# RetNet attention and squared-ReLU FFN on one core: the two row halves of a chunk ordered by TensorE's wait on itself, and three steps of an ending block left between the two parts of x

## The chip, the cores and the metric

The kernel runs on one core of a Trainium2 chip, in one launch. The metric is the device time in microseconds; the median of the runs shown counts. The profile is one profiled execution: its span, from the first to the last instruction, was 984.6 us, and that run's time was 986.41 us.

The engines are called by their names or as the profile has them: TensorE (PE for the matmuls, PEld for the loads of the stationary operand), VectorE (DVE), ScalarE (ACT), GpSimd (POOL) and SyncE (SP, whose queue issues nearly all DMAs).

## The reference

Batch 8, 8 heads, 576 positions, head size 64; then an FFN over 4608 tokens, 512 to 2048 to 512. q, k and v are float32, the weights float64 (the kernel rounds them itself), and the result is float32.

```python
scores = scale * np.matmul(q, k.transpose(0, 1, 3, 2))
Dmat = np.where(rel >= 0, gamma[:, None, None] ** rel[None, :, :], 0.0)
ret = scores * Dmat[None, :, :, :]
attn = np.matmul(ret, v)                 # (B, H, S, D)
x = attn.transpose(0, 2, 1, 3).reshape(B * S, H * D)
h = np.maximum(x @ w_in, 0.0)
out = h * h @ w_out
```

## The kernel before

**Two phases.** In the first phase the attention is computed chunk by chunk, and between the chunks the first product of the FFN, for blocks of 512 tokens, is worked off in small steps. In the second phase, from about 580 us on, only the second product of the FFN remains (`inner`, L1033). The change touches the first phase alone.

**Chunks.** A sequence of 576 positions is cut into four chunks of 128 and one of 64; there are 40 chunks, numbered i. A chunk of 128 has two halves h of 64 positions. The decay allows a recurrent form: within a half the masked scores are multiplied with v ("own", `own_of`, L566), what all earlier halves leave is kept as a 64x64 state u for each head ("grow", `grow_of`, L556, which accumulates in PSUM and is copied out to `u_sb` by `grown`, L491 on ScalarE), and q times that state is added (L609). The results of own and of L609 accumulate in the same PSUM tile, `x_ps`, which holds all heads of a chunk and has one buffer.

**Row halves.** All these matmuls are 64x64 and use TensorE as four tiles of 64x64. Which rows of the array a matmul uses is set by the partitions of its operands: for own it is half h of the positions (`rows(h)`), for L609 it is one of the two heads of a pair (`rows(e)`). [...] In `whole` (L587), which does one chunk from the eleventh on, the order is: own and grow of half 0 in two parts (`beside_each` with `(0, 2)` and then `(4, 6)`), half of the next chunk's scores (L451), the matmuls of L609, own and grow of half 1 `(0, 2)`, the other half of the next scores, own and grow `(4, 6)`. Two waits stand in it: the first matmul of L609 must come after the end of the first part of own, and the last part of own after the last matmul of L609. The wait is made by `seen` (L576) and `after` (L572): ScalarE copies one column of a small tile `mark` (L577) once the awaited matmul is done, and the later matmul waits for that copy.

**x and the blocks.** `x_out` (L532) copies a chunk's `x_ps` into `xT` (L544 on ScalarE). `xT` holds x transposed, for two blocks of 512 tokens at a time. A chunk can lie across a block's boundary: the boundaries at tokens 2048, 3072 and 4096 fall into the middle of a chunk, those at 2560 and 3584 between two chunks. Where a chunk lies across, there are two copies: the first completes block n and puts the steps of block n on the list, the second begins block n + 1. Block n + 1 lies where block n - 1 was, so before that copy the loop at L541 works off all steps that block n - 1 still has.

**Steps.** A block has 28 steps (`ffn_in`, L703): for each of four groups of weights the seven products of a Strassen-like scheme, j = 0 to 6, into the PSUM tiles h_a, h_b, h_c (L718). Each product is evacuated by ScalarE (L728, L734) or VectorE (L730, L732, L737, L741, L744, with the squaring L725), on GpSimd A11 is squared (L735), and the sums L658 and L659 and the write of g to DRAM (L660, on SP's queue) are put on a list and done one by one in later steps. The first step (j = 0) needs x as it is; the second needs T2, the second of four sums over x that VectorE makes in `sum_x` (L637): L644, L645, L646, L647. If block n + 1 has its x by then, one of the four is made in each of the steps j = 3, 4, 5 of block n's last group (L748); the rest, or all of them, at step 0 of block n + 1. VectorE further does a piece of the conversion of w_out (L201 to L248, loaded at L196, written at L281) in most steps.

**Pace.** `ffn` (L802) is called for each chunk and decides how many steps come before the next chunk: it interpolates between points of `PACE` (L796), pairs of tokens gone and steps done. In the steps it also issues the transposes of q and k for a chunk two further (`flips`, L398 on VectorE, which waits for the load of k, L148 and L150) and the copies of these into place (`move`, L410, with L413 on ScalarE). Before each chunk `move(C, i)` issues what that chunk still lacks.

**Order.** The program is scheduled by hand (`manual_schedule`): each engine does its instructions in the order of the Python code. A wait of one instruction holds all later ones on the same engine.

Of the kernel before, what the change touches and what calls it, by code (L numbers as in the profile page):

```python
# [9 lines left out]
F32 = mybir.dt.float32  # L10
# [5 lines left out]
C = 128  # L16
CH = C // 2
TOK = 512
# [22 lines left out]
def kernel(  # L41
# [33 lines left out]
    nc = tc.nc  # L75
# [10 lines left out]
    N_MP = N_M // 2  # L86
    N_MQ = N_M // 2
    N_BLK = n_tok // TOK
    NP = len(PRODUCTS)
# [4 lines left out]
    const = ctx.enter_context(tc.tile_pool(name="const", bufs=1))  # L94
# [226 lines left out]
            f and f()  # L321

    dv = only.tile([128, H, 2 * NCH], F32, name="dv")
    mark = const.tile([128, 2], F32, name="mark")
    nc.vector.memset(mark, 0.0)
    exp_bias = const.tile([128, 1], F32, name="exp_bias")
    nc.gpsimd.memset(exp_bias, -896.0 * 2.0 ** 23)
    idle, ident = (W[6][:, at:at + 128] for at in (2688, 2816))
# [30 lines left out]
    def rows(half, n=64):  # L359
        return slice(64 * half, 64 * half + n)  # L360
# [7 lines left out]
    def clears(half, bank):  # L368

        new = (half, bank) not in clean  # L370
        clean.add((half, bank))
        return new
# [10 lines left out]
    N_ONE = N_TURN - 1  # L383
# [26 lines left out]
    def move(count, i=N_CH):  # L410

        while moves and count and moves[0][0] <= i and (moves[0][1] <= done[0] or count == C):
            nc.scalar.copy(*moves.pop(0)[2:])  # L413
            count -= 1
# [15 lines left out]
    def scores(i, part=False):  # L430

        b_, ci, c0, cs = chunks[i]
        if i < N_EARLY:

            sc = [ps_f.tile([128, 512], F32, tag="f", name="sc_ps")[:, 0:256].rearrange("p (h t) -> p h t", h=HP) for e in range(2)]
        else:
            both = ps_t.tile([128, 2, 512], F32, tag="t", name="sc_ps")[:, :, 0:256].rearrange("p e (h t) -> p e h t", h=HP)
            sc = [both[:, e, :, :] for e in range(2)]
        st[i]["sc"] = sc
        st[i]["both"] = None if i < N_EARLY else both  # L440
        if part:
            return
        for hp in range(HP):
            score(i, hp)
        masked(i)

    def score(i, hp):
        for h in range(chunks[i][3] // CH):
            for e in range(2):
                t = slice(CH * h, CH * h + CH)  # L450
                nc.tensor.matmul(st[i]["sc"][e][rows(h), hp, :], lhsT=st[i]["kT"][rows(e), hp, t], rhs=st[i]["qT"][rows(e), hp, t],  # L451
                                 start=True, stop=True, skip_group_check=True)

    def masked(i):

        b_, ci, c0, cs = chunks[i]
        sc, both = st[i]["sc"], st[i]["both"]
        r = st[i]["ret"] = st[i]["kT"].rearrange("p (e a) (b t) -> p e (a b) t", e=2, b=2)
        if i < N_EARLY:
            for e in range(2):  # L460
                nc.vector.tensor_tensor(r[:cs, e, :, :], sc[e][:cs], msk[:cs, 0, :, :].to_broadcast([cs, HP, CH]), op=ALU.mult)
        else:
            nc.vector.tensor_tensor(r[:cs], both[:cs], msk[:cs].to_broadcast([cs, 2, HP, CH]), op=ALU.mult)
        if i < N_ONE:
            scale_v(i)
# [7 lines left out]
    def x_at(hp, b, h):  # L473
        return xp[0][rows(b), hp // 2, 0:256].rearrange("p (g t) -> p g t", g=2)[:, hp % 2, CH * h:CH * h + CH]
# [15 lines left out]
    def grown(i, h):  # L490
        nc.scalar.copy(u_sb[(2 * chunks[i][1] + h + 1) % 3], u_ps[0])  # L491
# [40 lines left out]
    def x_out(i, after):  # L532

        b_, ci, c0, cs = chunks[i]
        tok = b_ * S + c0
        at = tok
        p = xp[0][:, :, 0:256].rearrange("p a (g t) -> p a g t", g=2)
        while at < tok + cs:
            n = at // TOK

            while steps and steps[0][0] <= n - 2:  # L541
                step()
            end = min(tok + cs, (n + 1) * TOK)
            nc.scalar.copy(xT[n][:, :, at - n * TOK:end - n * TOK].rearrange("p (a g) t -> p a g t", a=2),  # L544
                           p[:, :, :, at - tok:end - tok])
            if at == tok:
                after()
            at = end
            if n_next[0] < N_BLK and (n_next[0] + 1) * TOK <= at:
                steps.extend(block_steps(n_next[0]))  # L550
                n_next[0] += 1
        st[i] = loaded[i] = None
# [3 lines left out]
    def grow_of(i, h):  # L556

        ci = chunks[i][1]
        if ci == 0 and h == 0:
            u_ps[0] = ps_u.tile([128, HP, D], F32, tag="u", name="u_ps")  # L560
        u = u_ps[0]
        return [lambda hp=hp, e=e, b=b: nc.tensor.matmul(
            u[rows(e), hp, :], lhsT=loaded[i][1][rows(h), 2 * hp + e, :], rhs=st[i]["vs"][rows(h), 2 * hp + b, :],
            start=(ci == 0 and h == 0 and hp == 0), stop=(hp == HP - 1), skip_group_check=True) for hp, e, b in HEADS]

    def own_of(i, h):  # L566
        s = st[i]
        return [lambda hp=hp, e=e, b=b: nc.tensor.matmul(
            x_at(hp, b, h), lhsT=s["vs"][rows(h), 2 * hp + b, :], rhs=s["ret"][rows(h), e, hp, :],
            start=clears(b, hp // 2), stop=False, skip_group_check=True) for hp, e, b in HEADS_1]  # L570

    def after(later, earlier):  # L572
        tc.add_manual_dep(later.ins, earlier.ins.name,
                          mybir.DependencyInfo(mybir.DependencyClass.Sync, mybir.DependencyReason.DATA), reason="row halves")

    def seen(done_):  # L576
        a = nc.scalar.copy(mark[:, 1:2], mark[:, 0:1])  # L577
        after(a, done_)
        return a

    def beside_each(own, grow, js):
        made = []
        for j in js:
            made.extend(f() for f in own[j:j + 2] + grow[j:j + 2])
        return made

    def whole(i):  # L587

        b_, ci, c0, cs = chunks[i]
        s = st[i]  # L590
        xp[0] = ps_x.tile([128, 2, 256], F32, tag="x", name="x_ps", padded_shape=[128, 2, 512])
        clean.clear()
        more = ci + 1 < NCH
        out_of, into = own_of(i, 0), grow_of(i, 1) if more else []
        f1 = seen(beside_each(out_of, into, (0, 2))[-1])
        beside_each(out_of, into, (4, 6))
        if more:
            grown(i, 1)
        if i + 1 < N_CH:
            scores(i + 1, True)  # L600
            score(i + 1, 0)
            score(i + 1, 1)
        f2 = None
        for h in range(cs // CH):
            if 2 * ci + h == 0:
                continue
            u = u_sb[(2 * ci + h) % 3]
            for hp, e, b in HEADS[0:2] + HEADS[4:6] + HEADS[2:4] + HEADS[6:8]:
                m = nc.tensor.matmul(x_at(hp, b, h), lhsT=u[rows(e), hp, :], rhs=s["qT"][rows(e), hp, CH * h:CH * h + CH],  # L609
                                     start=clears(b, hp // 2), stop=False, skip_group_check=True)  # L610
                if f1:
                    after(m, f1)
                    f1 = None
        if cs == C:
            f2 = seen(m)
        grows = i + 1 < N_CH and chunks[i + 1][3] == C
        out_of, into = own_of(i, 1) if cs == C else [], grow_of(i + 1, 0) if grows else []
        beside_each(out_of, into, (0, 2))
        if i + 1 < N_CH:
            score(i + 1, 2)  # L620
            score(i + 1, 3)
            masked(i + 1)
        last = beside_each(out_of, into, (4, 6))
        if f2:
            after(last[0], f2)
        x_out(i, lambda: grown(i + 1, 0) if grows else None)


# [149 lines left out]
    def block_steps(n):  # L778
        if n == 0:
            seconds = [(0, first_in, j, (1,)) for j in range(N_HALF)]  # L780
            return seconds + [(0, first_in, j) for j in range(N_HALF, N_W1)]
        return [(n, ffn_in, n, mp, j) for mp in range(N_MP) for j in range(NP)]

    def step():
        n, f, *args = steps.pop(0)
        done[0] += 1
        f(*args)
# [5 lines left out]

    HALF = C // 2
    N_0 = N_W1
    PACE = ((4 * TOK, N_0 + 2 * N_MP * NP), (5 * TOK - HALF, N_0 + 3 * N_MP * NP - 2),  # L796
            (6 * TOK, N_0 + 4 * N_MP * NP), (8 * TOK, N_0 + 6 * N_MP * NP), (9 * TOK, N_0 + 7 * N_MP * NP - 2))
    done = [0]
    gone = [0]
    behind = []  # L800
# [1 line left out]
    def ffn(i, half):  # L802
# [13 lines left out]
        if not behind:  # L816
            behind.append((gone[0] - HALF, done[0]))
        points = behind + [p for p in PACE if p[0] > behind[0][0]]
        want = points[-1][1]
# [378 lines left out]
```

## Time and profile before

| | us |
|---|---|
| median of 3 runs | 986.56 |
| lowest and highest | 984.46, 989.82 |
| span of the profiled execution | 984.6 |
| TensorE matmuls busy | 956.0 |
| weight loads busy | 858.1 |
| VectorE busy | 783.9 |
| ScalarE busy | 346.5 |
| GpSimd busy | 127.9 |

The profile's page has the busy time of each engine, the span in 40 slices, the DMA queues, the chain that ended last, the costliest groups of instructions and the DMA issues. Of a group it gives line, engine, operation, the tiles written and read with their shapes, the count, then the busy time and the mean of one, and the idle time just before with what ended it. Beside the page there are views on the trace: busy times by stretches, who waited for whom, and the instructions in order of time (start, length, engine, line, operation, tiles, count; in brackets the idle time before and what ended it). Rows of the timeline are merged: "x16" is sixteen instructions in a row, from the first's start to the last's end.

Two things to keep in mind. Matmuls are pipelined and their ends are modelled, so a matmul row can cover a short hole; the rows of weight loads show such a hole better. And the time of the whole is an average over stages: the first 127 us (weights converted, chunks one by one), the stage from 127 to 532 us in which `whole` runs, the rest of the first phase, and the second phase.

### The profile page before, as it was taken

Reading aid. Unit: us, or ns where it says so; the run is one execution under the profiler, and the core shown is the slowest. Engines: PE = TensorE matmul, PEld = TensorE weight load, DVE = VectorE, ACT = ScalarE, POOL = GpSimd, SP = SyncE. Lnnn points to the kernel's source line nnn. Section 1 sums busy time; section 2 is a strip of 40 time slices with the busy share of each in tenths; the row PEclk is TensorE's granted clock in tenths of the full one; section 3 lists DMA queues with packets and bytes.
Section 4 is the critical chain, followed back from the end, with each engine's and each line's share of the span. In section 5 each row is a group of like instructions: output and inputs, shape, how many; then the busy total and the mean of one; then the engine's idle time right before and its main releaser. Section 6 shows DMA issues by size and latency. Waiting matters only on the chain. (4 is left out here: it accounts for less than half of the span.)

```text
span 984.6 us, 24068 instructions
## 1 busy us (share of the span) xinstructions
PE 956.0 (97%) x10108; PEld 858.1 (87%) x10108; DVE 783.9 (80%) x1448; ACT 346.5 (35%) x872; POOL 127.9 (13%) x121
## 2 busy tenths in 40 slices
PE   7799989999999999999999999999999999999998
PEld 7645778888878878888788889999999999999998
DVE  4789779887897778878786577878878787787876
ACT  3454366665774856665651000000000000000000
POOL 3211223122122221321200000000000000000000
PEclk9999999999999999999999999999999999999999
DMA  8875537575746764596229976645352544534241
GB/s 203 235 216 156 160 99 208 155 246 187 219 141 214 214 192 146 153 290 190 84 104 377 345 257 240 232 152 200 109 204 108 183 178 170 202 126 171 87 172 44
DMA packets 172012, 181.43 MB, mean 184 GB/s; under 512 B 118144, under 2 KB 132480, under 8 KB 165248
## 3 DMA queue, kind: packets, MB, share of 16 engines
q1 hardware_dynamic: 169792, 179.38, 56.5%
q8 instruction: 79, 1.29, 0.5%
q10 hardware_dynamic: 2112, 0.52, 0.2%
q14 instruction: 29, 0.24, 0.1%
HBM read 109.36 MB, written 70.52 MB: 183 GB/s over the span
## 5 line engine op out<-in xcount | busy, mean ns | idle before, releaser
L718 PE MATMUL h_b<-room,w 128*128 128x256 f32 x768 | 185.7, 385 | 11.3 <-DVE room L645 7.9
L718 PEld LDWEIGHTS h_b<-room,w 128*128 128x128 f32 x768 | 146.1, 192 | 34.3 <-issue 9.8
L413 ACT COPY qk<-flip 32x256 f32<-32x256 f32 x416 | 167.3, 402 | 6.0
L1047 PE MATMUL o_b<-w,room 128*128 128x128 f32 x1168 | 144.4, 275 | 0.2 <-DVE room L999 0.2
L1047 PEld LDWEIGHTS o_b<-w,room 128*128 128x128 f32 x1168 | 137.2, 192 | 0.4 <-DVE room L999 0.4
L1047 PE MATMUL o_c<-w,room 128*128 128x128 f32 x1008 | 123.0, 275 | 0.0
L718 PE MATMUL h_a<-room,w 128*128 128x256 f32 x512 | 122.9, 383 | 0.0
L718 PE MATMUL h_c<-room,w 128*128 128x256 f32 x512 | 122.3, 382 | 0.0
L1047 PEld LDWEIGHTS o_c<-w,room 128*128 128x128 f32 x1008 | 117.7, 192 | 0.0
L1061 ACT COPY r<-o_a 128x128 f32<-128x128 f32 x53 | 14.1, 266 | 271.9 <-PE o_a L1047 236.2
L718 PEld LDWEIGHTS h_c<-room,w 128*128 128x128 f32 x512 | 97.6, 192 | 13.9 <-DVE room L744 0.2
L718 PEld LDWEIGHTS h_a<-room,w 128*128 128x128 f32 x512 | 95.7, 190 | 14.0 <-issue 0.5
L1047 PE MATMUL o_a<-w,a 128*128 128x128 f32 x688 | 85.6, 275 | 0.0
L1047 PEld LDWEIGHTS o_a<-w,a 128*128 128x128 f32 x688 | 81.2, 192 | 0.1
L725 DVE SCALAR_TENSOR_TENSOR room<-room 128x512 f32<-128x512 f32 x96 | 74.0, 770 | 3.3
L735 POOL TENSOR_TENSOR room<-room 128x512 f32<-128x512 f32 x32 | 34.4, 1076 | 319.6 <-ACT room L734 282.2
L682 PE MATMUL h_ps<-room,w 128*128 128x512 f32 (+1 forms) x152 | 58.9, 535 | 3.4 <-DVE w L228 2.5
L377 POOL TENSOR_TENSOR q_ld<-q_ld,dv 128x512 f32<-128x512 f32 (+1 forms) x39 | 43.3, 1109 | 112.4 <-DMA q_ld<-in_q_dram 87.4
L737 DVE TENSOR_TENSOR room<-h_b,room 128x512 f32<-128x512 f32 x32 | 22.0, 688 | 44.9 <-PE h_b L718 44.9
L470 POOL TENSOR_TENSOR v_ld<-v_ld,dv 128x512 f32<-128x512 f32 (+1 forms) x40 | 50.7, 1268 | 22.8 <-DMA v_ld<-in_v_dram 16.4
L682 PEld LDWEIGHTS h_ps<-room,w 128*128 128x128 f32 x152 | 27.6, 190 | 26.1 <-issue 23.3
L1047 PE MATMUL o_b<-w,a 128*128 128x128 f32 x344 | 45.6, 275 | 0.0
(112 smaller groups left out, 1389.0 us busy)
## 6 DMA issues: line engine op xcount, KB each, us to landing
g_dram<-room SPq DMA_DIRECT2D x32, 1280.0 KB, 5.5
a<-g_dram SPq DMA_DIRECT2D x30, 1024.0 KB, 6.0
room<-g_dram SPq DMA_DIRECT2D x15, 1024.0 KB, 6.0
w<-w_dram SPq DMA_DIRECT2D x7, 1792.0 KB, 10.5
out_dram<-room SPq DMA_DIRECT2D x17, 512.0 KB, 3.3
w<-in_moe_w_in_dram SPq DMA_DIRECT2D x16, 512.0 KB, 5.6
w<-in_moe_w_out_dram SPq DMA_DIRECT2D x16, 512.0 KB, 4.0
v_ld<-in_v_dram SPq DMA_DIRECT2D x31, 256.0 KB, 3.4
```

What stands on the lines that cost most here:

```text
L377: engine.tensor_tensor(t, t, dv[:cs, :, NCH + ci:NCH + ci + 1].to_broadcast([cs, H, D]), op=ALU.mult)
L413: nc.scalar.copy(*moves.pop(0)[2:])
L470: nc.gpsimd.tensor_tensor(vs[:cs], vs[:cs], dv[:cs, :, ci:ci + 1].to_broadcast([cs, H, D]), op=ALU.mult)
L682: nc.tensor.matmul(p.rearrange("p h t -> p (h t)"), lhsT=w[:, c, :], rhs=xT[0][:, c, lo * HT:hi * HT], start=(c == 0), stop=(c == N_DM - 1))
L718: nc.tensor.matmul(p[:, mm, :], lhsT=w[:, c, :], rhs=xs[n][right][:, c, :], start=(j in OPENS and mm == 0 and c == 0), stop=(j in CLOSES a ...
L725: nc.vector.scalar_tensor_tensor(t, t, 0.0, t, op0=ALU.max, op1=ALU.mult)
L735: nc.gpsimd.tensor_tensor(g["A11"], g["A11"], g["A11"], op=ALU.mult)
L737: nc.vector.tensor_tensor(g["A22"], p, p15, op=ALU.add)
L1047: nc.tensor.matmul(p, lhsT=s["lefts"][left][:, m, :], rhs=w_out[j][:, m, WO_SLOT[right], :], start=(i in OPENS and m == 0), stop=(i in CLO ...
L1061: nc.scalar.copy(r[:, 0, 0:128], p)
```

## The change

Three parts:

1. `seen`, `after` and the tile `mark` go. In their place `wait_for` (a `nop` on TensorE that depends on the awaited matmul) stands ahead of L609 and ahead of the last part of own. The awaited matmuls are the same as before.
2. The loop in `x_out` that works off an ending block now issues two copies (`move(2)`) before each step, for chunks from the eleventh on.
3. Three points of `PACE` change: at tokens 2048, 3072 and 4096 the steps wanted were all those of the ending block; now they are two fewer, and the point lies 16 tokens later. In the order of the built kernel this leaves the last three steps (j = 4, 5, 6) of blocks 2, 4 and 6 to the loop in `x_out`, between the two copies L544. The points for tokens 2560 (less 64) and 4608 are as before.

```diff
-    mark = const.tile([128, 2], F32, name="mark")
-    nc.vector.memset(mark, 0.0)
...
             while steps and steps[0][0] <= n - 2:
+                if i >= N_ONE:
+                    move(2)
                 step()
...
-    def after(later, earlier):
-        tc.add_manual_dep(later.ins, earlier.ins.name,
+    def wait_for(earlier):
+        tc.add_manual_dep(nc.tensor.nop().ins, earlier.ins.name,
                           mybir.DependencyInfo(mybir.DependencyClass.Sync, mybir.DependencyReason.DATA), reason="row halves")
-
-    def seen(done_):
-        a = nc.scalar.copy(mark[:, 1:2], mark[:, 0:1])
-        after(a, done_)
-        return a
...
-        f1 = seen(beside_each(out_of, into, (0, 2))[-1])
+        m = beside_each(out_of, into, (0, 2))[-1]
         beside_each(out_of, into, (4, 6))
...
-        f2 = None
+        wait_for(m)
         for h in range(cs // CH):
...
                 m = nc.tensor.matmul(x_at(hp, b, h), lhsT=u[rows(e), hp, :], rhs=s["qT"][rows(e), hp, CH * h:CH * h + CH],
                                      start=clears(b, hp // 2), stop=False, skip_group_check=True)
-                if f1:
-                    after(m, f1)
-                    f1 = None
-        if cs == C:
-            f2 = seen(m)
...
-        last = beside_each(out_of, into, (4, 6))
-        if f2:
-            after(last[0], f2)
+        if cs == C:
+            wait_for(m)
+        beside_each(out_of, into, (4, 6))
         x_out(i, lambda: grown(i + 1, 0) if grows else None)
...
-    PACE = ((4 * TOK, N_0 + 2 * N_MP * NP), (5 * TOK - HALF, N_0 + 3 * N_MP * NP - 2),
-            (6 * TOK, N_0 + 4 * N_MP * NP), (8 * TOK, N_0 + 6 * N_MP * NP), (9 * TOK, N_0 + 7 * N_MP * NP - 2))
+    PACE = ((4 * TOK + HALF // 4, N_0 + 2 * N_MP * NP - 2), (5 * TOK - HALF, N_0 + 3 * N_MP * NP - 2),
+            (6 * TOK + HALF // 4, N_0 + 4 * N_MP * NP - 2), (8 * TOK + HALF // 4, N_0 + 6 * N_MP * NP - 2),
+            (9 * TOK, N_0 + 7 * N_MP * NP - 2))
```

## The prediction

> **What bounds the kernel now.** I read the page first, then the busy times by stage, then the waits of TensorE, then the timeline around the two places that the diff touches.
>
> ```profile
> PE 956.0 (97%) x10108; PEld 858.1 (87%) x10108; DVE 783.9 (80%) x1448; ACT 346.5 (35%) x872; POOL 127.9 (13%) x121
> ```
>
> ```profile
> 127.00:532.00 405.00, 391.31 (x4679) 337.03 (x4678) 329.88 (x519) 250.86 (x618) 92.41 (x81) 0.99 0.62 187
> 600.00:984.60 384.60, 381.39 (x3413) 381.01 (x3412) 309.87 (x697) 31.94 (x120) 0.00 (x0) 1.00 0.44 157
> ```
>
> The columns after the length are PE, PEld, DVE, ACT and POOL busy, the clock, the DMA share and GB/s. TensorE sets the pace in both stages. From 600 us on its weight loads fill 99% of the time and nothing of the change is there. From 127 to 532 us, where the change is, loads fill 83%: there are holes. VectorE is busy 81% there, ScalarE 62%, so a hole that goes is worth its full length as long as VectorE keeps up.
>
> ```profile
> PE h_b L718 <- DVE room L645: 7.9, 4, 2.3
> ...
> PE x_ps L609 <- ACT mark L577: 2.1, 3, 1.2
> ```
>
> This is the waits of TensorE (total, times, longest). The first line has a block's second step waiting for a sum over x, at four block starts. The second is the wait that the change replaces; it looks small, because a 64x64 matmul is drawn 0.218 us long and covers the hole. The loads show it:
>
> ```profile
> 285.73 0.33 PEld L451 LDWEIGHTS sc_ps<-qk 64*64 64x64 f32 x16
> ...
> 285.86 0.19 ACT L577 COPY mark<-mark 128x1 f32<-128x1 f32 x1 [1.56 <-PE u_ps L562]
> 286.04 0.37 ACT L491 COPY u_sb<-u_ps 128x256 f32<-128x256 f32 x1
> 286.10 0.56 PEld L609 LDWEIGHTS x_ps<-qk,u_sb 64*64 64x64 f32 x32
> ...
> 286.79 0.33 PEld L451 LDWEIGHTS sc_ps<-qk 64*64 64x64 f32 x16
> ...
> 286.92 0.19 ACT L577 COPY mark<-mark 128x1 f32<-128x1 f32 x1 [0.50 <-PE x_ps L609]
> ...
> 287.16 0.14 PEld L568 LDWEIGHTS x_ps<-qk,v_ld 64*64 64x64 f32 x2
> ```
>
> The timeline (start, length): sixteen score loads end at 286.06; one load takes 0.135, so the last began at 285.93. The next begins at 286.10, 0.05 after the mark copy ends: 0.17 from load to load, where these forms otherwise come at most 0.04 apart. The same again at 287.16.
>
> ```profile
> 476.66 1.59 PEld L718 LDWEIGHTS h_a<-room,w 128*128 128x128 f32 x8
> ...
> 477.29 0.39 ACT L544 COPY room<-x_ps 128x256 f32<-128x256 f32 x1
> ...
> 479.46 0.65 DVE L644 TENSOR_TENSOR room<-room 128x512 f32<-128x512 f32 x1
> ...
> 480.14 0.69 DVE L645 TENSOR_TENSOR room<-room 128x512 f32<-128x512 f32 x1
> ...
> 480.95 2.35 PEld L718 LDWEIGHTS h_b<-room,w 128*128 128x128 f32 x7 [2.70 <-issue]
> 480.98 2.61 PE L718 MATMUL h_b<-room,w 128*128 128x256 f32 x6 [2.33 <-DVE room L645]
> ```
>
> A block start: its first step is done in 1.7 us, but L644 and L645 come behind a mask, a flip and leftovers of the old block on VectorE. And the seven loads after the hole take 2.35 us, eight before it 1.59: TensorE runs at half clock. Load by load, they come 0.427 apart instead of 0.216 for some 3.4 us after the holes at 355 and at 478 us.
>
> **What the Trainium skill says.** "PSUM — Partial Sum Buffer", section "PSUM bank collisions raise a hardware error": two row tiles must not write one PSUM bank at once, and software has to order them. That is why a wait must stay; no run here shows a collision. "Perfetto Trace Analysis", section "Tensor Engine Instruction (MATMUL, LD_WEIGHTS)": a matmul's shown end is estimated, its semaphore follows the acknowledged write. The trace agrees that holes hide: 2.1 us of waiting shown, 9.3 found below. "TensorE: Matmul & The Clock Gate", section "What's actually happening": the array falls to half clock after an idle window of about 3.4 us. Here it follows holes shown as 2.1 and 2.3 us idle; the measurement decides. "TensorEngine Tiling (Array Packing)", section "Key Properties": switching the tiling mode drains TensorE. The trace agrees: 0.52 us from the last 128-row load to the first 64-row one, against 0.216.
>
> **Part 1, the waits.** 54 mark copies go (30 chunks with a first wait, 24 with a second), with their 54 x 0.19 = 10.3 us of ScalarE, which is hidden. The order of the built kernel shows no instruction for the nop: its wait stands on the first matmul behind it, the one that waited for the mark before. I went through the 54 places load by load. 38 gaps are 0.15 to 0.18 (less 0.04, together 5.0 us), eight are longer (1.48, 1.01, 0.45, 0.39, 0.32, 0.32, 0.24, 0.23; together 4.1 over 0.04), eight are up to 0.12 (0.2): **9.3 us** of holes.
>
> What is put there? In 48 of the places the awaited matmul ends 0.22 us or more before the slot of the waiting load (in the six others a late mark hides where that slot was). From its end to the mark's start take 0.12, from the mark's end to the load 0.05. A wait without the copy has at most both legs, 0.17, less than 0.22: it costs nothing, and loads behind it don't queue. Not all comes back: at 175.7 and 436.0 us the mark was late because ScalarE still worked on other copies (until 176.94 and 436.84). L491 stands behind those, and the matmuls L562 must wait for it; moving that copy up by 0.19 gives 0.3 us there, and 1.15 and 0.65 stay. Gain 9.3 - 1.8 = **7.5 us**. TensorE's wait on itself right behind such a short stretch isn't in the trace: bounds are 9.3 (nothing stays), and 4.8 if each costs 0.05, one leg more. I take 7.5.
>
> **Part 2, the three steps.** Blocks 3, 5 and 7 begin inside a chunk. Now the ending block is finished before that chunk, both x copies L544 follow each other, and the new block's first step comes at once. The changed PACE leaves steps 4, 5, 6 of the old block between the copies: 3 x 1.73 = 5.2 us of TensorE work (1.73 from step to step), during which L644 and L645 are emitted (at step 4 and 5). The number of steps stays. The holes, load to load less 0.216: 233.1 us 1.79, 355.1 us 2.45, 478.1 us 2.68, together **6.9 us**. The fourth, 292.4 us (2.33), is at a block that begins with a chunk; its order is the same after the change, and I leave it.
>
> What waits then? From the end of step 4 to the second step of the new block VectorE has L737, L725, L644, a w_out piece, L741, L725, L645, a w_out piece, L744 (it frees h_b). Back to back their starts are 0.6 to 0.68 apart (0.35 for a piece of 0.42): about 5.2, 5.4 and 5.8 with the pieces that stand at the three places, against 5.2 of TensorE. About 0.2 + 0.4 + 0.8 = 1.4 us stay. Gain **5.5 us**, bounds 3.5 and 6.9.
>
> Half clock: both windows follow holes that go. (0.427 - 0.216) x 16 loads = **3.4 us**. Bounds 0 and 3.4.
>
> **What moves at no cost.** At three chunks the flips L398 come three steps (5.2 us) later; the copies from them serve a chunk two further. 18 copies L413 (3 x 3 x 2, 0.40 each) go ahead of those steps; the second L544 is behind six of them, and the next chunk's matmuls into x_ps are some four steps away. On SP's queue writes L660, w_out loads L196 and writes L281 swap places with loads by one group; on POOL three squares L735 swap with scalings (POOL 23% busy). One step before the chunk at 117 us goes behind it. There the flip L398 waited 4.9 us for k_ld, whose load stood behind a write L660 waiting for L659; work before L659 is the same, so the hole (3.6 us) stays, to within 1 us. The memset of mark is hidden behind the first load.
>
> Sum: 7.5 + 5.5 + 3.4 = **16.4 us** off a span of 984.6: 968.2. That run's time was 986.4 and the median is 986.56, so 986.6 - 16.4 = **970.2**.
>
> **Rivals.**
> - *The wait isn't hidden.* The self-wait costs what the mark did: part 1 gives nothing. 977.7. For it: no close self-wait in the trace. Against: 0.17 below 0.22.
> - *The block starts don't pay.* VectorE (81%) can't finish three steps and the sums in 5.2 us, and a hole of the same size and its half clock come back one step later. 986.6 - 7.5 = 979.1. For it: the 5.2 to 5.8 above. Against: then all delays would have to add up.
> - *Slower.* The self-wait drains TensorE like a mode switch: 0.52 from load to load, 0.48 too much. 54 x 0.48 = 25.9, with the 1.8 that stays 27.7 against 9.3 today: +18.4, less 8.9 of part 2: 996.1. It decides from 0.30 us a wait on (54 x 0.30 = 9.3 - 1.8 + 8.9). Against: 35 loads at L718 and L568 that wait on TensorE's own semaphore have the medians of loads without one (0.216 inside the FFN, 0.20 and 0.52 at the form switches); but what they wait for was long done.
> - *It does nothing*: holes just move to the next wait of each chunk. 986.
> - *All goes*, the 1.8, the 1.4 and the 2.3 at 292 us too: 970.2 - 5.5 = 964.7.
>
> **Numbers.** Forecast 0.58, the wait 0.11, block starts 0.14, slower 0.06, nothing 0.06, all 0.05. Range 964.5 to 980.5: it takes in all but the third and fourth rival (0.12), and the bounds of part 1 and of the half clock. Faster by over 0.5% (4.9 us, about what a measurement can tell): 0.58 + 0.11 + 0.14 + 0.05 = 0.88; within 0.06; slower 0.06.
>
> **What would show it.** (Lines as in the kernel before.) Right: gaps of 0.04 between loads ahead of L609 and L568, and no mark; no wait on the second x sum (L645) over 0.8 us but the one near 290 us; no loads 0.427 apart after a block start; VectorE over 82% busy in this stage. Wrong: gaps of 0.17 or more at the self-waits, TensorE waiting for L744 or L732 after a block start, or a longer wait for k_ld near 130 us.

## The result, and the profile after

The changed kernel took 974.95 us (median of four runs, 974.21 to 977.31) against 986.28 (four runs beside it): a ratio of 0.9885 with a 95% interval of 0.9853 to 0.9917, so 11.3 us faster. Forecast were 970.2, 16.4 us faster. A second measurement on another occasion gave 974.24 against 983.88, a ratio of 0.9892 (0.9862 to 0.9923), 10.6 us.

The page of the changed kernel gives the busy time of each engine, and the windows view the stage from 127 to 532 us (columns as before: length, PE, PEld, DVE, ACT and POOL busy, clock, DMA share, GB/s):

```profile
PE 952.2 (98%) x10108; PEld 856.3 (88%) x10108; DVE 783.0 (80%) x1447; ACT 338.4 (35%) x818; POOL 127.7 (13%) x121
```

```profile
127.00:532.00 405.00, 396.54 (x4729) 343.54 (x4728) 337.20 (x533) 246.34 (x570) 93.36 (x82) 1.00 0.65 196
```

ScalarE has 54 instructions fewer on the page. In the stage the loads fill 85% where they filled 83%, VectorE is busy 83% where it was 81%: more of the same work fits into the same stretch. From 600 us on the loads fill 99%, as before. This execution lost some 2 us ahead of the stage (its first own comes at 127.90 us, in a second execution at 125.66); where sums matter I use the second one too (span 973.0).

**The waits.** The timeline of the changed kernel around 287 us, the place that the prediction showed at 286 us:

```profile
286.86 0.33 PEld L449 LDWEIGHTS sc_ps<-qk 64*64 64x64 f32 x16
287.09 0.56 PEld L604 LDWEIGHTS x_ps<-qk,u_sb 64*64 64x64 f32 x32
287.22 0.37 ACT L489 COPY u_sb<-u_ps 128x256 f32<-128x256 f32 x1 [1.80 <-PE u_ps L562]
```

L604 (L609 before) now begins 0.04 us after the last of the sixteen scores, with no mark between; the gap was 0.17. At all 54 places the waiting load follows at its normal distance, 0.04 us or less, but for the last chunk's (0.11): there 0.34 us lie between the load of the awaited matmul and the waiting load, at the other places 0.45 or more.

**The block starts.** The waits view of the changed kernel (total, times, longest):

```profile
PE h_c L708 <- DVE room L722: 3.8, 1, 3.8
...
PEld h_b L708 <- DVE room L727: 2.0, 2, 1.1
PE h_b L708 <- DVE room L635: 1.9, 1, 1.9
```

The second sum over x (L635, L645 before) held TensorE four times, 7.9 us in all, and does so once now, at 293 us, where a block begins with a chunk. In its place shorter waits for evacuations have come, at the third of these starts for L727 (the other of the two times that the view gives for L727 is behind the flip shown further below). The timeline of the changed kernel there shows why:

```profile
484.37 0.69 DVE L396 STREAM_TRANSPOSE flip<-k_ld 64x512 f32<-64x512 f32 x1
484.99 0.64 DVE L727 TENSOR_TENSOR room<-h_b,room 128x512 f32<-128x512 f32 x1
...
485.69 1.59 PEld L708 LDWEIGHTS h_b<-room,w 128*128 128x128 f32 x8 [0.94 <-DVE room L727]
```

The sums are made in time, but a mask and a flip then stand ahead of L727, which empties h_b. The three holes of 1.79, 2.45 and 2.68 us are now 0.59, 0.31 and 0.91, and these eight loads take 1.59 us: full clock.

**What got worse.** The timeline of the changed kernel behind the flip that waits for k_ld:

```profile
133.39 1.70 PEld L708 LDWEIGHTS h_b<-room,w 128*128 128x128 f32 x8
...
137.94 0.71 DVE L396 STREAM_TRANSPOSE flip<-k_ld 128x512 f32<-128x512 f32 x1 [7.25 <-DMA k_ld<-in_k_dram]
138.58 0.65 DVE L722 TENSOR_TENSOR room<-h_c,room 128x512 f32<-128x512 f32 x1
...
139.28 2.12 PEld L708 LDWEIGHTS h_c<-room,w 128*128 128x128 f32 x8 [4.20 <-DVE room L722]
```

The flip waited 4.9 us before and 7.25 now. The hole of TensorE is 4.17 us (3.6 before), a second one of 1.22 follows at 141 us, and the eight loads take 2.12 us: part of them at half clock. And ahead of grow there is a new wait, seen in the timeline near 269 us:

```profile
266.92 1.24 ACT L411 COPY qk<-flip 32x256 f32<-32x256 f32 x3
...
268.18 0.72 ACT L218 ACTIVATE w<-w,exp_bias 128x512 uint32<-128x512 uint32 x1
268.81 0.65 ACT L219 ACTIVATE w<-w 128x512 f32<-128x512 uint32 x1
269.36 0.35 ACT L489 COPY u_sb<-u_ps 128x256 f32<-128x256 f32 x1
269.78 0.17 PEld L562 LDWEIGHTS u_ps<-v_ld,k_ld 64*64 64x64 f32 x2 [0.92 <-issue]
```

L489 copies u out of PSUM, and the next L562 may write there only after it. It ends at 269.71 because it queued behind three copies and a piece of the w_out conversion (L218 and L219); the load follows 0.07 later. The profile writes "issue", that is, it names nothing; I first took this for GpSimd (experiment e6).

**The sums.** From each trace I took, for the stretch from the first own to the last L604 (L609 before) load: the length of the 30 attention stretches (from the last step's load before a chunk to the first after it), the holes inside steps (load to load over 0.23 us, less 0.216), and what half clock costs (loads of steps 0.38 to 0.46 apart, less 0.216 each). The changed kernels have one step (1.73 us) more inside; "length" is without it, for a like comparison. Each row is one execution.

| us | length | attention | holes in steps | half clock |
|---|---|---|---|---|
| before | 403.4 | 82.7 | 14.1 | 3.3 |
| changed | 392.6 | 78.8 | 9.5 | 0.8 |
| changed, second execution | 392.3 | 79.2 | 8.3 | 1.2 |
| e1, waits alone (no step to take off) | 400.6 | 77.4 | 15.3 | 4.4 |
| e2, steps alone | 402.5 | 89.3 | 6.8 | 2.7 |
| e3, without the copies | 397.3 | 84.8 | 7.7 | 1.2 |
| e4, earlier load | 387.2 | 79.5 | 4.0 | 0.0 |
| e5, one PACE point more | 389.6 | 77.6 | 7.0 | 1.3 |
| e7, tight self-waits | 404.8 | 92.8 | 8.5 | 0.0 |
| e8, marks nobody waits for | 392.5 | 80.7 | 8.3 | 0.0 |
| last version | 382.5 | 76.5 | 2.1 | 0.0 |

### The profile page after: what moved, and what is told of

Read it like the earlier page. It is cut to its first block, busy times and chain, and to the rows that moved or that the text cites. A ratio compares the mean times of both kernels' runs of the same rounds, so it can differ in the third digit from the quotient of the medians.

```text
span 975.6 us, 24006 instructions
## 1 busy us (share of the span) xinstructions
PE 952.2 (98%) x10108; PEld 856.3 (88%) x10108; DVE 783.0 (80%) x1447; ACT 338.4 (35%) x818; POOL 127.7 (13%) x121
## 5 line engine op out<-in xcount | busy, mean ns | idle before, releaser
L411 ACT COPY qk<-flip 32x256 f32<-32x256 f32 x416 | 167.4, 402 | 8.5 <-DVE flip L396 2.3
L708 PEld LDWEIGHTS h_a<-room,w 128*128 128x128 f32 x512 | 96.5, 190 | 14.1 <-issue 0.5
L1052 ACT COPY r<-o_a 128x128 f32<-128x128 f32 x53 | 14.1, 265 | 271.7 <-PE o_a L1038 236.0
L715 DVE SCALAR_TENSOR_TENSOR room<-room 128x512 f32<-128x512 f32 x96 | 70.2, 731 | 3.3
L727 DVE TENSOR_TENSOR room<-h_b,room 128x512 f32<-128x512 f32 x32 | 22.0, 689 | 38.9 <-PE h_b L708 38.9
L468 POOL TENSOR_TENSOR v_ld<-v_ld,dv 128x512 f32<-128x512 f32 (+1 forms) x40 | 48.3, 1209 | 23.5 <-DMA v_ld<-in_v_dram 13.9
```

Of the source, the lines that this page charges most:

```text
L468: nc.gpsimd.tensor_tensor(vs[:cs], vs[:cs], dv[:cs, :, ci:ci + 1].to_broadcast([cs, H, D]), op=ALU.mult)
L708: nc.tensor.matmul(p[:, mm, :], lhsT=w[:, c, :], rhs=xs[n][right][:, c, :], start=(j in OPENS and mm == 0 and c == 0), stop=(j in CLOSES a ...
L715: nc.vector.scalar_tensor_tensor(t, t, 0.0, t, op0=ALU.max, op1=ALU.mult)
L727: nc.vector.tensor_tensor(g["A22"], p, p15, op=ALU.add)
L1052: nc.scalar.copy(r[:, 0, 0:128], p)
```

## The experiments

Times are medians; ratios are to the kernel before, run beside them, and gains over it in us are worked out from the ratios.

### e1: the waits alone

The changed `wait_for`, with PACE and the loop of the kernel before:

```diff
-                if i >= N_ONE:
-                    move(2)
                 step()
...
-    PACE = ((4 * TOK + HALF // 4, N_0 + 2 * N_MP * NP - 2), (5 * TOK - HALF, N_0 + 3 * N_MP * NP - 2),
+    PACE = ((4 * TOK, N_0 + 2 * N_MP * NP), (5 * TOK - HALF, N_0 + 3 * N_MP * NP - 2),
```

(and so for the other two points)

> Part 1 alone: TensorE's wait on itself in place of the mark copies; the points of PACE and the loop in x_out as before. My theory from the two traces: a short gap between loads overstates what a wait cost, because loads run ahead of their matmuls; each is worth about 0.07 us, not 0.13, but the holes behind late marks come back whole, and some new waits for GpSimd appear. Gain 4 to 7 us: 279 us range 979.5 to 982.5 (that is, 979.5 to 982.5 us against 986.3). The hole near 130 us stays at 3.6 us (if it grows here too, it is the waits and not the pace that did it). As forecast: 978.8 (7.5 off), the hole as before. Rival, the wait isn't hidden: 985.5 to 986.5.

(The "279 us range" is a slip; the range meant is the one in brackets.) Measured: 982.69, ratio 0.9968 (0.9954 to 0.9982), 3.2 us. Attention stretches fell by 5.3, but the hole near 130 us was 4.44 us and brought thirteen loads at half clock with it (2.7 us). So the wait is hidden, though the gain is below the 4 to 7 us that I expected, and that hole can be long without the new pace. The waits of TensorE for ScalarE's next copies (L489, L411) are there too at the old pace: their gaps over 0.04 add up to 2.6 us here, 0.4 before.

### e2: the steps alone

The new PACE and `move(2)`, with the marks (the edit is shown against the changed kernel):

```diff
-    def wait_for(earlier):
-        tc.add_manual_dep(nc.tensor.nop().ins, earlier.ins.name,
+    def seen(done_):
+        a = nc.scalar.copy(mark[:, 1:2], mark[:, 0:1])
+        after(a, done_)
+        return a
```

> Parts 2 and 3 alone: the new points of PACE and the two copies a step in x_out, with the mark copies and their waits as before. My theory: block starts give 5.1, half clock 3.4, the hole near 130 us takes 2.7 back: about 6 off, 979 to 981.5 us, with the hole near 130 us at about 6 us. As forecast: 8.9 off, 977.4, hole within 1 us of 3.6. Rival, block starts don't pay: 985 to 987. If this gain and that of the waits alone add up to the gain of the whole (11.3), the parts don't touch each other; if they add up to clearly more, the new waits for GpSimd and ScalarE are what they cost each other.

Measured: 982.58, ratio 0.9971 (0.9959 to 0.9983), 2.9 us: less than expected, though the holes in steps went from 14.1 to 6.8. The attention stretches took it back: 89.3 against 82.7. The timeline of e2 near 272 us shows how (L579 is the mark, L611 the waiting matmul):

```profile
271.45 0.72 ACT L218 ACTIVATE w<-w,exp_bias 128x512 uint32<-128x512 uint32 x1
...
272.07 0.64 ACT L219 ACTIVATE w<-w 128x512 f32<-128x512 uint32 x1
272.62 0.17 ACT L579 COPY mark<-mark 128x1 f32<-128x1 f32 x1
272.70 0.36 ACT L491 COPY u_sb<-u_ps 128x256 f32<-128x256 f32 x1
272.84 0.32 PEld L611 LDWEIGHTS x_ps<-qk,u_sb 64*64 64x64 f32 x16 [1.06 <-ACT mark L579]
```

The new pace puts other copies and pieces ahead of the marks on ScalarE, and each mark comes as late as its queue lets it. The gaps at the first wait, as far as over 0.04, add up to 11.2 us here, 6.8 before. So the two halves give 3.2 + 2.9 = 6.1 alone and 11.3 together: with the new pace the wait on itself saves 10.1 us of attention stretches (89.3 to 79.2), with the old one 5.3. The size of this is rough: e2's profiled execution took 985.24 us, 2.7 above its median.

### e3: without the copies ahead of the steps

```diff
             while steps and steps[0][0] <= n - 2:
-                if i >= N_ONE:
-                    move(2)
                 step()
```

> The changed kernel without the two copies ahead of each step in x_out. My theory: the copies then come only ahead of the next chunk, all at once, and the scores of the chunk wait for ScalarE there: 1 to 3 us slower than the changed kernel (976 to 978), with longer holes ahead of the scores at three chunks. Rival: ScalarE has time enough and the second part of x comes earlier without six copies ahead of it: the same or up to 1 us faster (974 to 975).

Measured: 980.03, ratio 0.9946 (0.9925 to 0.9967): about 5 us slower than the changed kernel, more than expected. The timeline of e3 after a block start (L449 is a score):

```profile
359.62 1.65 ACT L411 COPY qk<-flip 32x256 f32<-32x256 f32 x4
...
360.49 0.19 PEld L449 LDWEIGHTS sc_ps<-qk 64*64 64x64 f32 x2 [2.22 <-ACT qk L411]
```

The copies from the flip come all at once ahead of the next chunk, and its scores wait 2.3 and 0.7 us for them here and 1.1 and 0.7 at another block start, at 481 us. The two lines of `move(2)` are no ornament: without them the other parts give 5.3 of the 11.3 us.

### e4: one load earlier

```diff
+            if i == N_ONE:
+                load(i + 3, "qk")
             ffn(i - 1, 1)
...
-            if i == N_TURN - 1:
-                load(i + 3, "qk")
```

> The changed kernel with one load of q and k (for the chunk whose flips wait near 130 us) issued ahead of the steps of that iteration, so that it no longer stands on SP's queue behind a write of g that waits for VectorE; nothing else moves. My theory: the flip stops waiting (7.25 us today), and both holes behind it with their half clock, 6.3 us together, go: 3 to 6.5 us faster than the changed kernel, 968.5 to 972. Rival: the load is as late anyway, because it waits for its buffer or shares the queues with others: within 1 us of 975. Rival two: the time is given back at the next wait: 973 to 975 with the hole gone.

Measured: 970.02, ratio 0.9841 (0.9823 to 0.9860), 4 to 5 us faster than the changed kernel. Only SP's order differs: the load is ahead of the write L650, which waits for VectorE. In its timeline the flip no longer waits (no bracket):

```profile
129.28 0.70 DVE L396 STREAM_TRANSPOSE flip<-k_ld 128x512 f32<-128x512 f32 x1
```

The holes at 130 to 144 us and their half clock are gone and come back nowhere. So that place costs what the table says, and the load's position is its cause.

### The changed kernel again, e5 and e6

> The changed kernel once more, since it stands on four runs only and the two halves of the change gave 3.2 and 2.9 us against 11.3 for the whole. If the halves help each other (marks queue behind the copies that the new pace brings; e2's trace has 89.3 us of attention stretches against 82.7 before): 974 to 976 again. Rival, the 11.3 was luck of the four runs: 977.5 to 980, nearer the 6.1 that the halves add up to.

Measured: 974.24, ratio 0.9892 (0.9862 to 0.9923). That is 10.6 us, and the lower end of the interval, 7.6, lies above the 6.1 of the two halves: the gain of the whole was no luck.

e5 shifts one more point of PACE:

```diff
-(5 * TOK - HALF, N_0 + 3 * N_MP * NP - 2)
+(5 * TOK - HALF, N_0 + 3 * N_MP * NP - 4)
```

> The changed kernel with one more point of PACE shifted: the block that ends ahead of token 2560 keeps two steps more for the time after its successor's x is complete, so that three of the sums over x stand beside steps and not ahead of the first ones. My theory: the 2.22 us hole near 293 us (the one block start that the change doesn't touch) goes, because VectorE then makes the second sum before TensorE asks for it: 1.5 to 2.5 us faster than the changed kernel, 972.5 to 973.5. Rival: VectorE is as late, only elsewhere, and the two steps cost later: 974.5 to 976.

Measured: 971.74, ratio 0.9872 (0.9837 to 0.9906), 2.5 us faster than the 974.24 beside it. The two intervals overlap, but the traces agree on the size: the stage is 2.7 us shorter, and the hole of 2.22 us near 293 us is gone. The waits of scores for ScalarE went too (1.65 to 0.1), while the hole for L727 at 478 us rose from 0.9 to 1.7.

e6 changes GpSimd's order:

```diff
-                scale_v(i + 1)
...
+        if N_ONE <= i < N_CH - 2:
+            scale_v(i + 2)
```

> The changed kernel with GpSimd's order changed: the scaling of v for the next chunk but one is issued ahead of the scaling of q, which waits for a DMA. My theory: TensorE's new waits for GpSimd ahead of grow (2.15 us in the trace, one of 1.01) go: 1 to 2 us faster than the changed kernel, 973 to 974. Rival: the scaling of v waits for its own load as long: within 0.5 of the changed kernel.

Measured: 974.75, no gain. The scaling of v comes earlier, and yet the waits ahead of grow stay: 1.5 us (gaps over 0.04) of 2.1 in the second execution, the long one 0.51 instead of 1.02, those of 0.22 unchanged. The timeline of e6 at the long one:

```profile
266.48 1.06 POOL L468 TENSOR_TENSOR v_ld<-v_ld,dv 128x512 f32<-128x512 f32 x1 [6.74 <-DMA v_ld<-in_v_dram]
...
269.11 0.36 ACT L489 COPY u_sb<-u_ps 128x256 f32<-128x256 f32 x1
269.54 0.17 PEld L562 LDWEIGHTS u_ps<-v_ld,k_ld 64*64 64x64 f32 x2 [0.41 <-issue]
```

The scaling of v ends at 267.54 us, L489 at 269.47, and the load follows 0.07 later. My reading was wrong. The wait ahead of grow is for more than one engine and has two records in the trace: the load's own, and one of a semaphore instruction before it. In the second execution that one lasts 1.36 us from 265.83, until 267.19, and L489 ends at 267.15. Even in e5, where the profile puts this wait down to GpSimd (L468), the semaphore instruction ends 0.04 after L489.

### e7: what a self-wait costs uncovered

The wait is made for the matmul just ahead instead of the earlier one; what must be ordered is still ordered:

```diff
-            score(i + 1, 1)
+            m = score(i + 1, 1)
         wait_for(m)
...
-            score(i + 1, 3)
+            m = score(i + 1, 3)
```

> The changed kernel with TensorE's wait on itself made for the matmul just ahead (the last score) instead of the earlier one, at all places with scores between: what an uncovered self-wait costs. From the one place of the changed kernel with little between (the last chunk): 0.35 us from the awaited matmul's load to the waiting load, where 0.04 is normal, so 0.31 a wait; 53 waits: 14 to 17 us slower than the changed kernel, 989 to 992, slower than the kernel before. Rival, a self-wait costs nothing wherever it stands: 975. Rival two, it drains like a mode switch (0.48 a wait): 1000.

Measured: 987.46, ratio 1.0036 (1.0019 to 1.0052): 13.2 us slower than the changed kernel, and no better than the marks. The timeline of e7 (L605 is the waiting matmul):

```profile
287.36 0.33 PEld L449 LDWEIGHTS sc_ps<-qk 64*64 64x64 f32 x16
...
287.92 0.56 PEld L605 LDWEIGHTS x_ps<-qk,u_sb 64*64 64x64 f32 x32 [0.23 <-PE sc_ps L449]
```

The scores' last load begins at 287.55 (0.33 less 0.14 after 287.36) and the waiting load 0.37 later. All 53 waits have 0.33 to 0.38 there, 16.6 us of gaps over 0.04. The attention stretches grew by only 13.7, which is 0.26 a wait against 0.31 of gap. Part of the difference lies elsewhere, for the waits for L489 and L411 are 0.8 us shorter in e7. In the 20 chunks that have no such wait in either trace, 36 self-waits have 11.4 us of gaps over 0.04 and cost 10.0: 0.28 a wait (0.26 to 0.33 by the form of the chunk), and 0.04 of each gap is made up. That a load starts ahead of its matmul fits this: between the starts of the matmuls the gaps at the waits are 0.28 to 0.33 where they are 0.33 to 0.38 between the loads.

### e8: the copies without the wait

```diff
         m = beside_each(out_of, into, (0, 2))[-1]
+        seen(m)
...
+        if cs == C:
+            seen(m)
```

> The changed kernel with the mark copies put back at their places on ScalarE, where nothing waits for them any more: the copies without the wait. My theory now: ScalarE's queue is what TensorE meets next (the new waits ahead of grow are for the copy of u_ps, L489, not for GpSimd), so each dead copy ahead of that copy adds up to 0.19 us where it is late already; with 30 chunks that is at most 5.7 us, likely 1 to 4: 975.5 to 978.5. If the copies cost nothing, 974 to 975: then the whole gain of part 1 was the wait. Rival: copies were the cost, not the wait: 980 or more.

Measured: 973.64, ratio 0.9883 (0.9862 to 0.9904): no slower than the changed kernel. In its trace the attention stretches are 1.5 us longer (the waits ahead of grow 3.4 instead of 2.1), while no half clock follows the hole near 130 us in this execution, where it cost 1.2 in the other. So the copies may cost up to 1.5 us, which the medians can't tell from nothing. But for at most that much, the gain of part 1 comes from the wait that went, not from the 10.3 us of ScalarE.

### e9: relief for ScalarE

```diff
-            nc.scalar.activation(frac, lo, AF.Copy, scale=2.0 ** -52)
+            if j < N_W1:
+                nc.scalar.activation(frac, lo, AF.Copy, scale=2.0 ** -52)
+            else:
+                nc.gpsimd.tensor_scalar(frac, lo, 2.0 ** -52, None, op0=ALU.mult)
```

> The changed kernel with one of the two ScalarE instructions of each piece of w_out's conversion (the scaling of the low words, L219, 0.66 us) done by GpSimd. If TensorE's new waits (ahead of grow for the copy L489, ahead of scores for the copies L411) are for ScalarE's queue, the long ones, 1.02 and 0.88 us, shrink by about 0.66 each, and the time falls by 0.5 to 1.5 us: 972.8 to 973.8. Rival, the waits are for something else: they stay, 974 to 975. Risk: GpSimd is slower at it and VectorE waits for the piece; then new holes at evacuations and 975 to 985.

Measured: 974.67, ratio 0.9897 (0.9868 to 0.9926), no gain. The timeline of e9's ScalarE at the place of the new wait (L414 and L492 are L411 and L489):

```profile
266.36 1.24 ACT L414 COPY qk<-flip 32x256 f32<-32x256 f32 x3
267.76 0.72 ACT L218 ACTIVATE w<-w,exp_bias 128x512 uint32<-128x512 uint32 x1 [0.16 <-DVE w L210]
268.39 0.35 ACT L492 COPY u_sb<-u_ps 128x256 f32<-128x256 f32 x1
```

L219 is gone, the copies waited for come 0.6 to 1.0 us sooner after the chunk's first matmul, and the two long waits shrink from 1.02 to 0.35 and from 0.88 to 0.29. That is the size of L219: the wait is for ScalarE's queue. The time didn't follow. In this trace the attention stretches are 2.1 us shorter than in the second execution, but the holes in steps 1.5 longer, since VectorE fell behind: in the same stage it is busy for 344.3 us instead of 337.2, with one instruction more, and TensorE has holes of 0.76 and 1.06 at 233 and 239 us for its sum over x and an evacuation, where one of 0.60 stood. GpSimd takes 1.65 us for a piece; whether VectorE's instructions are longer because GpSimd works beside them I haven't tried.

### Together

The earlier load and e5's point:

> The earlier load and the shifted point of PACE together, on the changed kernel: each took its own hole away (4.2 and 2.5 us off). If they don't touch each other: 967 to 968.5. Rival, one gives part of the other back (the new schedule needs the load at another time): 969.5 to 971.

Measured: 966.70, ratio 0.9813 (0.9791 to 0.9835): within what two runs can tell, they add up. Then with the points at tokens 2048 and 4096 at -3 instead of -2, so that four steps stand between the copies of x:

> As the last one, with the points of PACE at tokens 2048 and 4096 one step lower still: four steps of the ending block between the two copies instead of three, so that three of the sums over x stand beside steps. My theory: the rest of the holes at these block starts, for VectorE's evacuation of h_b (0.6 and 0.9 to 1.7 us), goes, 1 to 2 us: 965.5 to 967. Rival: eight copies ahead of the second copy of x and one step more of squares on VectorE take it back: 967.5 to 969.

Measured: 964.74, ratio 0.9791 (0.9770 to 0.9812), 21 us faster than the kernel before and about 10 faster than the changed one. The last step, 2.0 us, is within the two intervals; in the traces it shows as a stage 1.8 us shorter. The windows view of this last version, same stage:

```profile
127.00:532.00 405.00, 403.84 (x4770) 351.68 (x4762) 347.29 (x544) 246.13 (x568) 93.99 (x81) 1.00 0.67 203
```

The loads fill 87% and VectorE is busy 86%.

## Why the prediction came out as it did

The mechanism was right and the time lies in the range, but the gain was 11.3 us and not 16.4. The range was 16 us wide and took in the rivals of 977.7 and 979.1 as well, so the time alone would not have told them apart; the traces and experiments do. By its steps, with the second execution for sizes:

- **Part 1, "Gain 9.3 - 1.8 = 7.5 us": attention stretches fell by 3.6**, below both bounds given (4.8 and 9.3). Two terms were mis-sized. First, 9.3 took each gap between loads at face value. In the 20 chunks that have no other wait, before or after, 7.5 us of gaps brought 6.1: 0.04 of a gap is made up, for 54 places an estimated 2.1 us too much. Second, "1.8 stays" was thought of as two late marks. The mechanism named there is the right one: behind the mark TensorE meets ScalarE's next copy (L489, then L411). But it meets it at more places: the waits for L489 and L411 (gaps over 0.04) rose from 0.4 to 3.7 us, by 3.3. Of this rise e1 has 2.2 at the old pace already; the other 1.1 come with the new pace, which moves copies on ScalarE. 9.3 - 2.1 - 3.3 is 3.9, of 3.6 measured. That a wait without the copy is free (0.17 below 0.22) held: no gap at the places, but for the 0.07 of the last chunk.
- **Part 2, 5.5 us: 5.1 measured** (6.9 of holes, now 1.8). The residues 0.2 + 0.4 + 0.8 were estimated; measured are 0.59 (h_b's evacuation by L720), 0.31 (an h_a that ScalarE empties) and 0.91 (h_b's evacuation by L727). The half clock behind these starts is gone, 3.1 of 3.4 (fifteen loads, not sixteen).
- **"The hole (3.6 us) stays, to within 1 us": it failed.** With its second hole and half clock it costs 5.5, 1.9 more (6.3 in the first execution), and the longer wait for k_ld came, which the prediction had named as a sign of being wrong. The step said that "work before L659 is the same". True, but the chunk now begins one step sooner: the write L650 is issued 0.1 us before the chunk's first own instead of 1.56 before, and the load stands behind that write. So TensorE reaches the flip's step sooner and the load doesn't. e1, whose pace is the old one, has a long hole too (4.44), and there the write is issued 1.05 before: the waits seem to have a part in it, though with one execution each this isn't shown. e4 shows that the load's place is what it hangs on.
- **"What moves at no cost"**: 18 copies L413 ahead of the steps were costed at nothing as a burden. As a whole they are no burden: e3 shows that they save some 5 us.
- Small holes and single slow loads that I had not counted (0.54 at 152 and 0.48 at 218 us among them) gave about 1.5.

So 3.6 + 5.1 + 3.1 - 1.9 + 1.5 = 11.4, of 11.1 in the stage.

The parts aren't independent, which the sum took for granted: alone they give 3.2 and 2.9. I had summed the marks' gaps in the trace of before, at the old pace; at the new one, in e2, those of the first wait are 4.4 us larger.

Of the rivals: "the wait isn't hidden" and "the block starts don't pay" fall by the traces and by e1 and e2. "Holes just move to the next wait" came true in part: 3.3 us of them did. "Slower" decided from 0.30 us a wait; e7 shows that a self-wait without cover is just there (0.31 of gap, 0.28 of time) and takes the gain away. It was the distance from the awaited matmul that kept this rival from coming true. The 0.48 of the prediction, taken from a mode switch, was too high.

## What to carry to other kernels

A wait that goes by way of another engine costs what is queued on that engine at the time, so its price changes with every change of that queue. TensorE's wait on itself cost 0.26 to 0.33 us here where nothing stood between, and nothing where 0.45 us or more lay between the two loads. When a wait by way of another engine is removed, look one instruction further for what the same queue delivers next. And when a chunk is moved ahead of a step, ask of each load that it needs soon whether the load moved too.

## What the runs showed that I had not expected

- **Gaps between weight loads overstate a hole.** At the marks the gap was 0.172 between loads but 0.117 between the starts of the matmuls, where 0.038 is normal; in e7's undisturbed chunks 0.32 of gap over 0.04 is 0.28 of time.
- **Half clock doesn't follow from a hole's length alone.** The Trainium skill ("TensorE: Matmul & The Clock Gate", section "What's actually happening") speaks of an idle window of about 3.4 us. Holes of 2.45, 2.68 and 2.79 us were followed by seven or eight loads at 0.427 us, one of 4.44 by thirteen; holes of 3.6 (before), 3.29 (e8) and 2.59 us (e1) by none. I don't know what decides.
- **A uint32 to float32 scaling of 128x512** took GpSimd 1.65 us (e9) and ScalarE 0.67 (the changed kernel).
